# A router's first round on full arrays, and the order of the work behind it

## The chip, the cores and the metric

The kernel runs on one core of a Trainium2 chip. The metric is the device time of one execution in microseconds (us), as the median of several runs.

## The reference

Three layers follow each other on 4608 tokens. Attention with 32 memory slots per head gives x (4608 x 512). A mixture of eight experts follows: all (token, expert) scores are sorted, and each token goes to its best expert that still has room (576 tokens each). A dense layer pair with a gated ReLU6 ends the work.

```python
logits = x @ w_gate
for idx in np.argsort(-logits.flatten()):
    tok, e = idx // E, idx % E
    if assigned[tok] >= 0 or counts[e] >= cap:
        continue
    assigned[tok] = e; counts[e] += 1
for e in range(E):
    h = np.maximum(x[assigned == e] @ w1[e], 0.0)
    out[assigned == e] = h @ w2[e]
h = out @ w_in
y = (h * np.clip(h + 3.0, 0.0, 6.0) / 6.0) @ w_out
```

## The kernel before

Attention runs to about 190 us. It leaves the scores LG on the chip (128 partitions x 36 columns x 8 experts). The attention output x is written to memory as 36 tiles of 128 tokens. Eleven are done inside attention, and the other 25 by `x_tiles`, one half tile (one matmul group of 256 columns) at a time. Each finished tile is copied by ScalarE and written by SyncE's queue.

**The router** runs in eight rounds (`route(k)`), and each closes one expert. A round finds the expert that fills up first and the score at which it does. For that it searches the score's 32 bits in 8 steps of 4 bits (`for i in range(NST)`). In each step `cmp` (VectorE) marks in C which token's best score reaches which of 15 thresholds. TensorE multiplies C with the one-hot of the best expert, Bo, and so counts tokens per threshold and expert. FL says which counts reach 576, a matmul with ones broadcasts it, and VectorE makes the next thresholds. In round 0 the counting takes 36 matmuls, one for each token column, with 15 columns of the array. In later rounds it takes five matmuls over eight token columns each, with 128 columns. These leave an 8 x 8 block per pair of token columns, of which VectorE keeps the diagonal (CM, CR), and a further matmul with S8 folds it. After the search the round sums over partitions (`ce`, `tot`), turns every token's slot into a one-hot (`oh`, 36 columns in six pieces), and multiplies the pieces with token numbers to get the index list IDX. In round 0 VectorE makes five pieces and GpSimd the sixth (`ohp`). The x halves that remain are spread between those steps.

**Experts.** `weights` loads W1 and W2 of each expert (tensor number T, four chunks, by GpSimd's indirect DMA), squares them on ScalarE for a scale, and splits each into two half-precision tensors (ScalarE and VectorE). `gathers` fetches an expert's tokens, transposes them on TensorE (`xp`) and splits them (`xt`). `l1` is the first matmul layer, in groups of 48 matmuls over four banks for expert 0; `l2` is the second. A scale that all partitions need goes through `all_max`, a small matmul (`amx`) which takes one of the same four banks ("mm"). Experts go in pairs; `l34` then runs the dense layers for the pair's 1152 tokens.

**Dense weights** (32 pieces of 512 KB, 64-bit floats) are converted in the background by VectorE, ScalarE and GpSimd (tile `cva`): two pieces at a time, and four once expert 1's tokens are there (`spare`).

**What sets the order.** Every engine runs its list in order. The lists come from a small scheduler in the program itself: a clock `CK.now` that each matmul advances by a written cost, estimated busy times for VectorE, ScalarE and GpSimd (`V_.t`, `A_.t`, `G_.t`), and tasks that give up control until a time on this clock (`yield V_.t + HOP + LATE`). A time added to a `yield` makes no engine wait; it puts what follows later in the lists, behind whatever was written meanwhile. `need(cond)` lets the main line stand until a task has done its part; `l1` needs the expert's tokens, `l2` its second weights. On the chip an engine does wait where its next instruction's operand isn't there, and all behind it in its list waits too.

Of the kernel before, what the change touches and what calls it, by code (L numbers as in the profile page):

```python
# [9 lines left out]
F32 = mybir.dt.float32  # L10
# [10 lines left out]
def attn_moe_kernel(ctx: ExitStack, tc: tile.TileContext, q, k, v, phi, w_gate, w1, w2, w_in, w_out, out):  # L21
# [607 lines left out]

    MMQ = []  # L630

# [65 lines left out]
    def all_max(m, f, late=0.0):  # L697
        yield V_.t + HOP + late
        done = [False]
        while len(MMQ) >= 4 and not MMQ[0][0]:  # L700
            yield CK.now + 0.05
        p = mm_tile([128, 128], "amx", done)
        nc.tensor.matmul(p, m.bitcast(F32).to_broadcast([128, 128]), ident, start=True, stop=True)
        CK.now += 0.22
        yield CK.now + HOP
        V_.tensor_reduce(f, p, axis=AX.X, op=OP.max)
        done[0] = True

    def pow2(src, name, sq, lo, target, late=0.0):
# [11 lines left out]
        yield from all_max(m, f, late)  # L721
        SR[0] = SR[0] or sq
        f = f.bitcast(I32)
# [10 lines left out]
    IDX, EIX, SX = {}, {}, {}  # L734
    OHP = [False]
    SR = [False]
    R_OK = [0]
# [8 lines left out]
    def route(k):  # L746
        LATE = 0.0 if k < 2 else 1.6
        V = rt.tile([128, NT], F32, name="V")
# [3 lines left out]
        def best(c0, c1):  # L752
            n = c1 - c0
            L, v, b1, m = LG[:, c0:c1], V[:, c0:c1], B1[:, c0:c1], bm[:, c0:c1]
            V_.tensor_reduce(v, L, axis=AX.X, op=OP.max)
            V_.tensor_tensor(b1, L, v[:, :, None].to_broadcast([128, n, E]), op=OP.is_equal)
            V_.tensor_tensor(b1, b1, wE[:, None, :].to_broadcast([128, n, E]), op=OP.mult)
            V_.tensor_reduce(m, b1, axis=AX.X, op=OP.max)
            V_.tensor_tensor(Bo[:, c0:c1], b1, m[:, :, None].to_broadcast([128, n, E]), op=OP.is_equal)

        def cmp(C, TH, c0, c1):
# [8 lines left out]
        else:  # L770
            TH = TH0
            for i in range(NST):
                p = ps.tile([128, 64], F32, name="rtp")
                if k == 0:
                    due = []
                    for c0, c1 in ((0, 34), (34, NT)) if i == 0 else ((0, 18), (18, NT)):
                        if i == 0:
                            best(c0, c1)
                        cmp(C, TH, c0, c1)
                        due.append((c0, c1, V_.t))  # L780
                    if i > 1:
                        post()
                    if EM and i:
# [3 lines left out]
                        early()  # L787
                    x_tiles(3 if i else 4)
                    for c0, c1, v in due:
                        yield v + HOP  # L790
                        for t in range(c0, c1):
                            nc.tensor.matmul(p[:15, :E], C[:, t, 0:15], Bo[:, t], start=(t == 0), stop=(t == NT - 1))
                        CK.now += 0.0243 * (c1 - c0)
                    V_.t = max(V_.t, CK.now + HOP)
                    p1 = p
                else:
                    cmp(C, TH, 0, NT)
                    if i > 1:
                        post()
                    yield V_.t + HOP + LATE / 2  # L800
                    for t in range(0, NTP, 8):
                        nc.tensor.matmul(p, C[:, t:t + 8].rearrange("p t n -> p (t n)"),
                                         Bo[:, t:t + 8].rearrange("p t e -> p (t e)"),
                                         start=(t == 0), stop=(t == NTP - 8))
                    CK.now += 0.14
                    yield CK.now + HOP
                    V_.tensor_tensor(CM, p.rearrange("p (t e) -> p t e", t=8),
                                     MK[:, :, None].to_broadcast([128, 8, E]), op=OP.mult)
                    with nc.allow_low_precision(reason="integers up to 1152"):
                        V_.tensor_reduce(CR, CM.rearrange("p t e -> p e t"), axis=AX.X, op=OP.add)  # L810
                    yield V_.t + HOP + LATE / 2
                    p1 = ps.tile([128, 64], F32, name="rtp")
                    nc.tensor.matmul(p1[:, :E], S8, CR, start=True, stop=True)
                    CK.now += 0.03
                    yield CK.now + HOP
                r = slice(0, 128 if k else 15)
                V_.tensor_scalar(FL[r], p1[r, :E], float(CAP), None, op0=OP.is_ge)
                if k == 0:
                    x_tiles(1)
                yield V_.t + HOP  # L820
                p2 = ps.tile([128, 64], F32, name="rtp")
                nc.tensor.matmul(p2[:, :E], onesb[r], FL[r], start=True, stop=True)
                CK.now += 0.03
# [63 lines left out]
        if k == 0:  # L887
            x_tiles(4)
        yield V_.t + HOP + LATE
# [45 lines left out]
        def oh(q4):  # L935
# [3 lines left out]
            return o  # L939
        yield V_.t - 0.3  # L940
        OH = [oh(0)]
        if k == 0:
            lof = hbuf(2)[:, 0:6]
            G_.tensor_copy(lof, lo[:, 30:36])
            ohp = hbuf(1).bitcast(BF16)[:, 0:768].rearrange("p (t n) -> p t n", t=6)
            for t in range(6):
                G_.tensor_scalar(ohp[:, t], i128, lof[:, t:t + 1], None, op0=OP.is_equal)
            G_.t += 1.4
            OHP[0] = True
            x_tiles(7)  # L950
        for q4 in range(6):
            yield (G_ if k == 0 and q4 == 5 else V_).t + HOP + LATE
            if k == 0 and q4 == 4:
                OH.append(ohp)
            elif q4 < 5:
                OH.append(oh(q4 + 1))
            elif k:
                update()
# [5 lines left out]
            if k == 0:  # L964
                x_tiles(2 * NT if q4 == 2 else 2)
        yield CK.now + HOP
# [26 lines left out]
    def weights():  # L993
        for T in range(2 * E):
# [3 lines left out]
            for c in range(4):  # L998
                if T == 0 and c == 2:
                    while not OHP[0]:  # L1000
                        yield CK.now + 0.1
                w_issue(T, c)
                yield CK.now + 0.8, G_
# [14 lines left out]
            yield V_.t + HOP  # L1018
            s = yield from pow2(s4, f"s{which}_{k}", True, 0, (4, 13)[which], 1.5 if k > 1 else 0.0)
            (S1, S2)[which][k] = s  # L1020
# [44 lines left out]
    def gathers():  # L1065
        for k in range(E):
# [24 lines left out]
            for i in range(depth):  # L1091
                if k == 0 and i == 2:
                    while not SR[0]:
                        yield CK.now + 0.1
                fetch(i)
# [5 lines left out]
            for i in range(5):  # L1101
# [3 lines left out]
                done = [False]  # L1105
                while len(MMQ) >= 4 and not MMQ[0][0]:
                    yield CK.now + 0.05
# [154 lines left out]
    def x_tiles(n):  # L1262
        for _ in range(n):
# [7 lines left out]
            x_mm(t, ps, "mm", g)  # L1271
            CK.now += 0.435
            if g:
                x_ev(t)
                A_.t = max(A_.t, CK.now) + 0.5
                XC[0][0] = True
# [6 lines left out]
    def l1(k, carry=()):  # L1283
# [3 lines left out]
        for j0 in range(0, 8, G1):  # L1287
            need(lambda: k in XT)
            ps1 = []
            for j in range(j0, j0 + G1):  # L1290
                t = hbuf(j).bitcast(F16).rearrange("p (a n) -> p a n", a=2)
                HT[k].append(t)
                for a in range(2):
                    done = [False]
                    ps1.append((j, a, t, done, mm_tile([128, 288], "p1", done)))
                    if G1 == 1:
                        l1_mm(k, ps1, carry)
            if ps1:
                l1_mm(k, ps1, carry)
# [244 lines left out]
```

## Time and profile before

| | |
|---|---|
| median of 3 runs | 1480.12 us (1479.44 to 1480.93) |
| profiled execution | 1486.13 us, span 1484.3 us |
| TensorE matmul busy | 1368.3 us (92% of the span) |
| VectorE, ScalarE, GpSimd busy | 857.7, 731.7, 514.0 us |
| chain that ended last | TensorE 64%, VectorE 19%, waiting for nothing shown 6%, ScalarE 5% |

A busy time is the sum of an engine's instructions. The granted clock is the share of TensorE's full 2.4 GHz; 0.50 is its lower level, 1.2 GHz. In a timeline a line is an instruction or several merged ones (x6), with start, time from first to last, engine, source line, and in brackets how long the engine stood idle before and what released it. L619 and L568 are helpers that record most matmuls and most other instructions, so the tiles' names tell them apart.

### The profile page before, as it was taken

How to read it: one execution, taken by the hardware profiler on the slowest of the kernel's cores; microseconds unless marked ns; L12 is line 12 of the kernel's file. 1: busy time of each engine (PE TensorE's matmuls, PEld its weight loads, DVE VectorE, ACT ScalarE, POOL GpSimd, SP SyncE). 2: the span in 40 equal slices, each digit the busy share in tenths (PEclk: the TensorE clock that was granted, in tenths of full speed). 3: DMA queues.
4: the chain of work that ended last, by engine and by line, in shares of the span. 5: the costliest groups of instructions: out<-in, count | busy, mean ns of one | idle time of the engine just before them, and what ended most of it. 6: DMA issues, size and time to landing. Idle time of an engine off the chain costs nothing.

```text
span 1484.3 us, 25639 instructions
## 1 busy us (share of the span) xinstructions
PE 1368.3 (92%) x10170; PEld 925.4 (62%) x10170; DVE 857.7 (58%) x2018; ACT 731.7 (49%) x1419; POOL 514.0 (35%) x577
## 2 busy tenths in 40 slices
PE   4778785888899999999999999999999999999997
PEld 3667664767544555887555558885555589755553
DVE  4688966889997676652246766522469445221111
ACT  3677656559665364552334645524336545233332
POOL 5676304044465352310233523102335420023232
PEclk9999987899999999999999999999999999999999
DMA  9875486355420130320001303200013211000000
GB/s 296 297 252 193 138 257 229 120 177 174 141 85 22 48 120 1 107 65 1 1 22 57 111 1 107 65 1 1 22 48 120 72 51 50 1 1 22 1 22 22
DMA packets 65912, 130.65 MB, mean 88 GB/s; under 512 B 5248, under 2 KB 35968, under 8 KB 65792
## 3 DMA queue, kind: packets, MB, share of 16 engines
q1 hardware_dynamic: 49808, 74.48, 15.4%
q0 software_dynamic: 15168, 52.96, 11.0%
q8 instruction: 80, 1.31, 0.4%
q10 hardware_dynamic: 816, 1.57, 0.3%
q14 instruction: 40, 0.33, 0.1%
HBM read 110.12 MB, written 18.87 MB: 87 GB/s over the span
## 4 chain that ended last, share of the span: by engine, by line
PE 64%; DVE 19%; issue 6%; ACT 5%; DMA 3%; POOL 3%; ACTq 0%; SPq 0%; POOLq 0%; DVEq 0%
PE p L619 38%; PE acc L619 18%; DVE cva L568 4%; DVE w L568 2%; PE xa L420 2%; DMA xg<-xd,ix 2%; DVE h L568 1%; DMA wst<-in_moe_w_dram,ei 1%; POOL h L568 1%; PE kvp L191 1%; DVE ql L330 1%; PE xp L624 1%; ACT w L568 1%; ACT h L568 1%; DVE OH L568 1%
## 5 line engine op out<-in xcount | busy, mean ns | idle before, releaser
L619 PE MATMUL acc<-wo,h 128*128 128x512 f16 x1728 | 415.5, 380 | 8.3 <-DVE y L568 3.7
L619 PE MATMUL p<-yt,wi 128*128 128x384 f16 x2304 | 412.1, 327 | 0.0
L568 POOL TENSOR_TENSOR h<-h,h 128x384 f16<-128x384 f32 x192 | 187.0, 975 | 607.9 <-ACT h L568 466.3
L619 PEld LDWEIGHTS <-w 128*128 128x128 f16 x3072 | 339.5, 122 | 50.8 <-DVE w L568 5.3
L619 PEld LDWEIGHTS <-wi 128*128 128x128 f16 x2304 | 220.9, 98 | 162.7 <-issue 4.0
L619 PEld LDWEIGHTS <-h 128*128 128x128 f16 x1728 | 163.9, 98 | 178.6 <-issue 6.3
L568 ACT ACTIVATE h<-p,half_c,inv 128x384 f32<-128x384 f32 (+1 forms) x256 | 143.8, 587 | 265.5 <-PE p L619 262.1
L568 DVE SCALAR_TENSOR_TENSOR h<-h,p 128x384 f32<-128x384 f32 x192 | 105.7, 551 | 261.6 <-ACT h L568 258.6
L619 PE MATMUL p<-xt,w 128*128 128x288 f16 x1536 | 200.7, 290 | 2.5 <-DVE h L568 2.2
L619 PE MATMUL p<-h,w 128*128 128x288 f16 x1536 | 196.8, 288 | 5.0 <-DVE w L568 4.5
L568 ACT ACTIVATE h<-h 128x384 f16<-128x384 f32 x192 | 99.9, 521 | 131.0 <-DVE h L568 127.2
L568 POOL DMA_INDIRECT wst<-in_moe_w_dram,ei x64 | 71.1, 1110 | 119.2 <-DVE tot L568 36.3
L568 DVE SCALAR_TENSOR_TENSOR w<-wst,s,w 128x512 f16<-128x512 f32 x124 | 98.1, 823 | 1.0 <-ACT w L568 1.0
L568 DVE SCALAR_TENSOR_TENSOR h<-p,h 128x288 f16<-128x288 f32 x128 | 57.4, 453 | 64.2 <-ACT h L568 64.1
L568 ACT ACTIVATE h<-p 128x288 f16<-128x288 f32 x128 | 51.5, 408 | 86.9 <-PE p L619 86.9
L568 ACT ACTIVATE w<-wst,s 128x512 f16<-128x512 f32 x124 | 82.4, 712 | 7.0 <-DVE s L568 6.2
L568 DVE SCALAR_TENSOR_TENSOR cva<-dst,cva 128x512 int32<-128x512 int32 (+1 forms) x96 | 85.6, 915 | 0.4
L568 DVE TENSOR_REDUCE ym<-y 128x1 f32<-128x288 f32 x64 | 28.8, 449 | 92.7 <-ACT y L568 92.7
L568 ACT ACTIVATE wscr<-wst 128x1024 bf16<-128x1024 f32 x64 | 67.4, 1053 | 17.9 <-DMA wst<-in_moe_w_dram,ei 17.3
L568 ACT ACTIVATE y<-p 128x288 f32<-128x288 f32 x64 | 26.0, 407 | 99.7 <-PE p L619 98.9
L568 POOL DMA_INDIRECT xg<-xd,ix x35 | 35.9, 1026 | 70.6 <-PE xp L624 32.0
L191 PE MATMUL kvp<-kvt,A 128*64 128x128 f32 x576 | 43.6, 304 | 8.8 <-ACT A L170 4.2
(317 smaller groups left out, 1594.5 us busy)
## 6 DMA issues: line engine op xcount, KB each, us to landing
dst<-in_moe_w_out_dram SPq DMA_DIRECT2D x26, 512.0 KB, 3.7
qt<-in_q_dram SPq DMA_DIRECT2D x8, 1024.0 KB, 11.8
dq<-in_moe_w_in_dram SPq DMA_DIRECT2D x16, 512.0 KB, 4.9
xd<-xs SPq DMA_DIRECT2D x32, 256.0 KB, 4.5
kvt<-in_k_dram SPq DMA_DIRECT2D x7, 1152.0 KB, 9.6
kvt<-in_v_dram SPq DMA_DIRECT2D x7, 1152.0 KB, 11.9
dst<-in_moe_w_in_dram SPq DMA_DIRECT2D x15, 512.0 KB, 4.1
ph<-in_phi_dram SPq DMA_DIRECT2D x8, 576.0 KB, 10.6
```

Of the source, the lines that this page charges most:

```text
L191: nc.tensor.matmul(p[i * 64:(i + 1) * 64, g, 0:128], A[:, hp, r, :], KV[b][:, :, hp, r * 64:(r + 1) * 64], start=(r == 0), stop=(r == R - 1))
L330: nc.vector.scalar_tensor_tensor(QL[u][:, hs], QP[t], sq, QH[u][:, hs], op0=OP.mult, op1=OP.subtract)
L420: nc.tensor.matmul(p[r, g], AT[u][:, half, g, r], VB[b][:, g], start=True, stop=True)
L568: r = f(*a, **kw)
L619: nc.tensor.matmul(o, l, r, start=start, stop=stop)
L624: nc.tensor.transpose(o, i, idn)
```

## The change

- Round 0 counts as the later rounds do: five matmuls (`count`), CM and CR on VectorE, and the fold with S8.
- Each search step of round 0 issues six x halves (four, one and one; seven in the first step) where it issued four. Two stand behind the search, so none are left for the one-hots.
- All six one-hot pieces of round 0 are VectorE's. The waits on GpSimd's piece (`OHP`) and on the first scale (`SR`) go.
- `LOCK`: while `l1` of expert 0 takes its four banks, no scale and no token transpose takes one; and it starts when the first weight chunk is there.
- Round 1 gets later places: 0.4 more at two points in each search step, 2.4 at the sums and the first one-hot, 1.0 at each further one. Its one-hots come after expert 0's W2 is written. Expert 1's third to fifth gather wait for its first weights' chunks.
- The matmul of every weight scale comes 1.5 later; before, only from expert 2 on.
- The scheduler's costs of an x half and of its copy change (0.435 to 0.28; 0.5 to 1.05).

```diff
     def all_max(m, f, late=0.0):
-        while len(MMQ) >= 4 and not MMQ[0][0]:
+        while LOCK[0] or len(MMQ) >= 4 and not MMQ[0][0]:
             yield CK.now + 0.05
...
     def route(k):
-        LATE = 0.0 if k < 2 else 1.6
+        LATE, LS = ((0.0, 0.0), (2.4, 0.4), (1.6, 0.8))[min(k, 2)]
...
+        def count(p, c0, c1):
+            for t in range(c0, c1, 8):
+                nc.tensor.matmul(p, C[:, t:t + 8].rearrange("p t n -> p (t n)"),
+                                 Bo[:, t:t + 8].rearrange("p t e -> p (t e)"), start=(t == 0), stop=(t == NTP - 8))
+                CK.now += 0.028
...
-                    for c0, c1 in ((0, 34), (34, NT)) if i == 0 else ((0, 18), (18, NT)):
+                    for c0, c1 in ((0, 32), (32, NT)) if i == 0 else ((0, 16), (16, NT)):
...
-                    x_tiles(3 if i else 4)
+                    x_tiles(4 if i else 5)
                     for c0, c1, v in due:
                         yield v + HOP
-                        for t in range(c0, c1):
-                            nc.tensor.matmul(p[:15, :E], C[:, t, 0:15], Bo[:, t], start=(t == 0), stop=(t == NT - 1))
-                        CK.now += 0.0243 * (c1 - c0)
+                        count(p, c0, c1)
                     V_.t = max(V_.t, CK.now + HOP)
...
+                V_.tensor_tensor(CM, p.rearrange("p (t e) -> p t e", t=8),
+                                 MK[:, :, None].to_broadcast([128, 8, E]), op=OP.mult)
+                with nc.allow_low_precision(reason="integers up to 1152"):
+                    V_.tensor_reduce(CR, CM.rearrange("p t e -> p e t"), axis=AX.X, op=OP.add)
+                if k == 0:
+                    x_tiles(1)
+                yield V_.t + HOP + LS
+                p1 = ps.tile([128, 64], F32, name="rtp")
+                nc.tensor.matmul(p1[:, :E], S8, CR, start=True, stop=True)
...
         V_.tensor_copy(tot, sc[:, :, NT - 1])
         if k == 0:
-            x_tiles(4)
+            x_tiles(2)
...
+        while k == 1 and 0 not in W2:
+            yield CK.now + 0.1
         OH = [oh(0)]
         if k == 0:
-            lof = hbuf(2)[:, 0:6]
-            G_.tensor_copy(lof, lo[:, 30:36])
-            ohp = hbuf(1).bitcast(BF16)[:, 0:768].rearrange("p (t n) -> p t n", t=6)
-            for t in range(6):
-                G_.tensor_scalar(ohp[:, t], i128, lof[:, t:t + 1], None, op0=OP.is_equal)
-            G_.t += 1.4
-            OHP[0] = True
             x_tiles(7)
         for q4 in range(6):
-            yield (G_ if k == 0 and q4 == 5 else V_).t + HOP + LATE
-            if k == 0 and q4 == 4:
-                OH.append(ohp)
-            elif q4 < 5:
+            yield V_.t + HOP + (1.0 if k == 1 and q4 else LATE)
+            if q4 < 5:
                 OH.append(oh(q4 + 1))
...
     def weights():
-                if T == 0 and c == 2:
-                    while not OHP[0]:
-                        yield CK.now + 0.1
...
-            s = yield from pow2(s4, f"s{which}_{k}", True, 0, (4, 13)[which], 1.5 if k > 1 else 0.0)
+            s = yield from pow2(s4, f"s{which}_{k}", True, 0, (4, 13)[which], 1.5)
...
     def gathers():
             for i in range(depth):
-                if k == 0 and i == 2:
-                    while not SR[0]:
-                        yield CK.now + 0.1
+                while k == 1 and i > 1 and WC.get(2, (0,))[0] < i // 2:
+                    yield CK.now + 0.1
                 fetch(i)
...
     def x_tiles(n):
-            CK.now += 0.435
+            CK.now += 0.28
             if g:
                 x_ev(t)
-                A_.t = max(A_.t, CK.now) + 0.5
+                A_.t = max(A_.t, CK.now) + 1.05
...
     def l1(k, carry=()):
             need(lambda: k in XT)
+            need(lambda: k or 0 in WC)
+            LOCK[0] = k == 0
             ps1 = []
...
+            LOCK[0] = False
             if ps1:
                 l1_mm(k, ps1, carry)
```

## Rows read from the trace of the kernel before

**Rows 1.** The page, part 2: granted TensorE clock in 40 slices, tenths.
```profile
PEclk9999987899999999999999999999999999999999
```

**Rows 2.** Busy by stretch: length, engines, clock, DMA share, GB/s; sum: 242 to 445.
```profile
329.00:385.00 56.00, 51.45 (x400) 44.47 (x399) 54.46 (x98) 44.42 (x88) 23.26 (x19) 0.94 0.57 188
385.00:445.00 60.00, 50.96 (x260) 26.41 (x258) 59.38 (x90) 41.70 (x74) 35.72 (x25) 0.91 0.32 97
sum 203.00, PE 166.20 PEld 123.11 DVE 186.23 ACT 131.62 POOL 84.89; mean PE 33.24 PEld 24.62 DVE 37.25 ACT 26.32 POOL 16.98
...
700.00:800.00 100.00, 99.67 (x588) 53.53 (x587) 40.27 (x109) 38.32 (x73) 28.42 (x31) 1.00 0.02 9
```

**Rows 3.** Timeline, one warm search step of round 0.
```profile
222.47 1.05 PE L792 MATMUL rtp<-Bo,C 128*15 128x8 bf16 x36
...
224.09 0.17 PE L822 MATMUL rtp<-FL,onesb 15*128 15x8 bf16 x1
224.19 1.56 PE L420 MATMUL xa<-vb,ats 128*128 128x256 f32 x6
...
225.68 1.05 PE L792 MATMUL rtp<-Bo,C 128*15 128x8 bf16 x36
```

**Rows 4.** Timeline, the same chain in round 1; last, its five counting matmuls.
```profile
249.46 0.21 DVE L568 TENSOR_TENSOR CM<-rtp,MK 128x64 f16<-128x64 f32 x1
...
249.71 0.26 DVE L568 TENSOR_REDUCE CR<-CM 128x8 f16<-128x64 f16 x1
...
250.03 0.19 PE L813 MATMUL rtp<-CR,S 128*128 128x8 f16 x1 [2.99 <-DVE s_0m L568]
...
250.26 0.17 DVE L568 TENSOR_SCALAR FL<-rtp 128x8 bf16<-128x8 f32 x1 [0.23 <-PE rtp L813]
...
272.29 0.32 PE L802 MATMUL rtp<-Bo,C 128*128 128x64 bf16 x5 [1.00 <-DVE C L568]
```

**Rows 5.** Stretches of half a microsecond in round 0's search, columns as in rows 2.
```profile
199.00:199.50 0.50, 0.50 (x22) 0.43 (x19) 0.47 (x5) 0.00 (x0) 0.00 (x0) 0.79 1.05 426
...
209.50:210.00 0.50, 0.50 (x15) 0.35 (x15) 0.00 (x0) 0.25 (x1) 0.00 (x0) 0.97 0.65 49
```

**Rows 6.** Timeline, round 0 after its search: sums and one-hots.
```profile
231.11 0.17 DVE L568 CAST tot<-scn 128x2 bf16<-128x2 f32 x1
...
232.49 0.21 PE L891 MATMUL rtp<-tot,tri 128*128 128x2 bf16 x1
...
234.66 7.06 POOL L568 TENSOR_SCALAR h<-i,h 128x128 bf16<-128x128 bf16 x6
...
235.00 4.61 DVE L568 TENSOR_TENSOR OH<-lo,i 128x768 bf16<-128x768 int32 x5
...
241.78 0.18 PE L961 MATMUL rtp<-RH,h 128*128 128x10 bf16 x1 [0.40 <-POOL h L568]
```

**Rows 7.** Timeline, start of expert 0's layer one: gather, weight split, matmul.
```profile
245.55 1.17 POOL L568 DMA_INDIRECT h<-xd,ix  x1 [1.30 <-DVE bm L568]
...
251.50 2.56 ACT L568 ACTIVATE w<-wst,s 128x512 f16<-128x512 f32 x4 [2.14 <-DVE s L568]
...
260.24 0.32 PE L619 MATMUL p<-xt,w 128*128 128x288 f16 x1
```

**Rows 8.** Timeline, TensorE in expert 0's layer two, VectorE's last token split.
```profile
312.97 0.31 PE L961 MATMUL rtp<-RH,OH 128*128 128x10 bf16 x6 [2.73 <-DVE dmm L568]
...
321.32 0.63 PE L624 MATMUL xp<-ident,xg 128*128 128x128 f32 x4 [1.42 <-DMA xg<-xd,ix]
...
328.64 0.48 DVE L568 SCALAR_TENSOR_TENSOR xt<-xp,sx,xt 128x256 f16<-128x256 f32 x1 [0.25 <-ACT xt L568]
...
330.87 3.96 PE L619 MATMUL p<-xt,w 128*128 128x288 f16 x31
```

**Rows 9.** Timeline, TensorE at expert 1's layer two and the first dense layers.
```profile
361.93 23.85 PE L619 MATMUL p<-h,w 128*128 128x288 f16 x175 [4.15 <-DVE w L568]
...
396.50 0.77 PE L703 MATMUL amx<-ident,sy_1m 128*128 128x128 f32 x2 [5.84 <-DVE sy_1m L568]
```

More of the change, by code (lines that the diff above doesn't have):

```diff
@@ L628, in fp16 @@
         return max(0.027, n / 2400.0 + 0.003)
-    MMQ = []
+    MMQ, LOCK = [], [False]
     def mm_slot(done):
@@ L721, in pow2 @@
         yield from all_max(m, f, late)
-        SR[0] = SR[0] or sq
         f = f.bitcast(I32)
@@ L734, in attn_moe_kernel @@
     IDX, EIX, SX = {}, {}, {}
-    OHP = [False]
-    SR = [False]
     R_OK = [0]
@@ L787, in route @@
                         early()
-                    x_tiles(3 if i else 4)
+                    x_tiles(4 if i else 5)
                     for c0, c1, v in due:
                         yield v + HOP
-                        for t in range(c0, c1):
-                            nc.tensor.matmul(p[:15, :E], C[:, t, 0:15], Bo[:, t], start=(t == 0), stop=(t == NT - 1))
-                        CK.now += 0.0243 * (c1 - c0)
+                        count(p, c0, c1)
                     V_.t = max(V_.t, CK.now + HOP)
-                    p1 = p
                 else:
@@ L799, in route @@
                         post()
[L800 to L805, printed above, removed]
-                    yield CK.now + HOP
[L807 to L814, printed above, removed]
+                    yield V_.t + HOP + LS
+                    count(p, 0, NT)
+                    yield CK.now + HOP
+                V_.tensor_tensor(CM, p.rearrange("p (t e) -> p t e", t=8),
[4 more added lines that the diff above has]
+                    x_tiles(1)
+                yield V_.t + HOP + LS
+                p1 = ps.tile([128, 64], F32, name="rtp")
+                nc.tensor.matmul(p1[:, :E], S8, CR, start=True, stop=True)
+                CK.now += 0.03
+                if k == 0:
+                    V_.t = max(V_.t, CK.now + HOP)
+                else:
                     yield CK.now + HOP
-                r = slice(0, 128 if k else 15)
-                V_.tensor_scalar(FL[r], p1[r, :E], float(CAP), None, op0=OP.is_ge)
+                V_.tensor_scalar(FL, p1[:, :E], float(CAP), None, op0=OP.is_ge)
                 if k == 0:
@@ L821, in route @@
                 p2 = ps.tile([128, 64], F32, name="rtp")
-                nc.tensor.matmul(p2[:, :E], onesb[r], FL[r], start=True, stop=True)
+                nc.tensor.matmul(p2[:, :E], onesb, FL, start=True, stop=True)
                 CK.now += 0.03
@@ L964, in route @@
             if k == 0:
-                x_tiles(2 * NT if q4 == 2 else 2)
+                x_tiles(2 * NT)
         yield CK.now + HOP
@@ L1105, in gathers @@
                 done = [False]
-                while len(MMQ) >= 4 and not MMQ[0][0]:
+                while LOCK[0] or len(MMQ) >= 4 and not MMQ[0][0]:
                     yield CK.now + 0.05
```

## The prediction

> **What bounds the kernel now.** I read the 40-slice page first: the granted clock is below full only in the sixth to eighth slice, 186 to 297 us [rows 1]. Then the table by stage [rows 2]: from 700 us on TensorE is busy 99.67 of 100 us, so a delay or gain made earlier is simply carried to the end. From 242 to 445 us VectorE is busy 186.23 of 203 us, and 59.38 of 60 in the last part. So two things can move the total: when the first router round hands over (about 242 us), and how much of 242 to 445 VectorE (16.8 us idle) and TensorE (36.8 us idle) lose by waiting for each other. Last I read the timeline there, instruction by instruction.
>
> All arithmetic is on the profiled execution: 1486.13 us, span 1484.3. The median of the runs shown is 1480.12, that is 6.0 us (0.4%) less; I carry the difference over to the median.
>
> **First round, search steps.** A warm step runs from one block of 36 counting matmuls (1.05 us) to the next: 225.68 - 222.47 = 3.21 us [rows 3]. TensorE has no gap in it: six matmuls, which are three x halves, take 1.56 us, so a half is 0.52 and four are 2.08. The new step has six halves and a longer chain. Counted from the broadcast matmul of the flags: 0.10 for that, four halves 2.08, five wide counting matmuls 0.32, then the two new VectorE operations until the folding matmul starts, 250.03 - 249.46 = 0.57, then folding matmul 0.23 and flags 0.15 with a handover of 0.2, together 0.58, beside which the half queued behind the folding matmul runs [rows 4]. Sum 3.65, against 3.21: +0.45. Ends: 3.5 if TensorE never waits for the fold, 3.9 if each half is in the way. Seven steps: +3.2 (2.0 to 4.8). VectorE's dense maximum and the new thresholds stay beside the four halves. The DMAs grow to three 256 KB x writes and one 512 KB load a step, 1.28 MB in 3.65 us or 350 GB/s, below the 426 GB/s that one half microsecond shows [rows 5]; SyncE's queue gets the x writes sooner, each behind the load that waits for VectorE, as now. The first step gets the same fold and one more half in the stretch of low clock: +1.0.
>
> **Clock.** It falls to half at about 199.3 us and comes back at 209.5 [rows 5], although TensorE worked all that time; the 36 matmuls that use 15 columns are part of what it did. With full arrays it may come back sooner. No row shows by how much; the ends are 0 and one warm step's work, 3.2. I take half, -1.6, as nothing lies nearer.
>
> **Tail of the first round.** The prefix matmul starts at 232.49, 1.2 us after its operand ended (231.11 + 0.17), because four slow x halves are queued ahead. After the change one half is left, which runs in the pause before: -1.0. The one-hots: GpSimd's six end at 241.72 and the last matmul of the round starts at 241.78, while VectorE was done with five at 239.61 [rows 6]. At 0.92 each a sixth there ends at 240.5: -1.2. The Trainium skill, page "Perfetto Trace Analysis", section "Optimizing Scalar/DVE Operations", says that work may be better off on another engine when VectorE is saturated. By it the sixth one-hot would cost 0.9 instead of giving 1.2. The trace differs: VectorE stands idle from 239.61, so at this place it isn't saturated.
>
> Sum of the first round: 3.2 + 1.0 - 1.6 - 1.0 - 1.2 = +0.4, so its index is ready at about the same time (-3 to +3). Six halves a step only change where the x work stands.
>
> **Start of layer one.** What changes is behind the index. Two of four weight loads of expert 0 no longer wait for the one-hots, and the last x tile is written earlier, some 7 us by my sum. The first token gather starts at 245.55 [rows 7], 3 us after the index; now it starts directly: -2.5. The scaled weights start at 251.50, released by a scale that waited for those late loads. That wait goes, and VectorE's update and next best-expert pass (some 3 us) are next ahead of it, then the scale's matmul, now queued 1.5 us later: -1.5. Layer one's first matmul, 260.24, needs both; with gathers and conversions less bunched I take -4 (ends -1.5 and -6).
>
> **Layers of expert 0.** The second round's one-hots, scale matmuls and token transposes sit in TensorE's queue among layer two, and where their operand is late the layer waits behind them: 2.73 and 1.42 us are the large ones [rows 8]. Queued later, these go; keeping the four banks of layer one together saves about as much again at the scale matmul that now takes one of them. One-hots behind the second weights help these too. The lock itself only orders: a scale or transpose comes after the four banks are taken, at worst one group of 48 matmuls later (6.1 us at 3.96 / 31 [rows 8]), and nothing on another engine stands behind it. The new guard on expert 1's third to fifth gather holds GpSimd's list, with expert 1's second weight loads behind it; their conversion is over by then, so it costs nothing, or up to 3 us if not. Together -4 (ends 0 and -7). Layer two of expert 0 would end at 330.9 - 8 = 323.
>
> **What is late next.** The same delays put expert 1's tokens off. The last token split ends at 328.64 + 0.48 = 329.1, 1.7 us before layer one of expert 1 starts at 330.87 [rows 8]: there is no slack. The diff adds, in the scheduler's time, 2 x 0.4 in each of 8 steps, 2 x 2.4 at the two sums, 2.4 + 5 x 1.0 at the one-hots: 18.6 us. The whole frame stands 8 us earlier, so the tokens are ready at 329.1 + 18.6 - 8 = 340, and TensorE waits 17 us from 323. Layer one of expert 1 starts 9 us later than before. Ends: 0 (the delays elapse while VectorE is behind anyway) and +13.
>
> **What is paid back.** While TensorE waits, VectorE converts dense weights, which otherwise hold up the next stages. Layer two of expert 1 waits 4.15 us for its weights and the dense layers 5.84 for a scale queued on VectorE [rows 9]; each is followed by a stretch at the lower clock. A granted 0.94 over 56 us and 0.91 over 60 [rows 2] are 6.7 and 10.8 us at half, which lose 3.4 and 5.4. With 9 us more both waits go nearly whole, and with them I count half of that loss: 4.2 + 4.8 + 4 = 13; smaller waits in the dense layers, 1. So 9 - 14 = -5 (ends -12 and +9). In VectorE's terms: its idle time shrinks from 16.8 to about 12, which is what lay idle around those late one-hots. From 460 us on nothing differs, but for scales of the first two experts queued 1.5 later, which costs nothing where TensorE has other matmuls ahead.
>
> Forecast: 1480.1 - 5 = 1475 (1481 for an execution like the profiled one).
>
> **Rivals.** *The wait isn't paid back (slower).* While expert 1's tokens are missing, only two conversion buffers are free, so VectorE may idle along with TensorE. Then 9 us of delay stand against 4.2 + 2 for the weights at most, or against nothing where these, loaded after the gathers, slide along: +3 to +9, 1486. It decides from the point where VectorE is busy under some 70% of TensorE's wait. For it: the buffers, and no slack in rows 8. Against it: 186 of 203 us busy, with low-priority work always at hand.
>
> *No wait arises.* VectorE's queue runs behind the scheduler's clock already (the 5.84 us), so the added delays may elapse without being seen. Then -8 is carried, and some of the later waits shrink: -11, 1469. Against it: 18.6 is much more than any lag in the rows.
>
> *It cancels.* VectorE sets the pace to 445 us whatever TensorE does, and its work after the handover is the same; its idle time stays near 16.8. Then 1480. For it: 59.38 of 60 us busy. This also covers a change that doesn't do what it says: a search 0.45 us a step longer, with the clock coming back as late as before.
>
> **Numbers.** Forecast case (-3 to -8, so 1472 to 1477) 0.40; no wait 0.16; cancels 0.20; not paid back 0.24. A measurement of this kernel can tell 0.2%, 3 us, from no change. Faster 0.56, same 0.20, slower 0.24. The range takes in most of the outer cases: 1467 to 1486.
>
> **What would show it.** Search steps of 3.6 to 3.7 us with six halves; the clock back before 209; last one-hot matmul near 240.7; first token gather right behind the index, layer one near 256; no 2.7 us wait in layer two of expert 0; then a wait of 10 to 20 us before layer one of expert 1, with VectorE over 80% busy in it; the two waits of rows 9 under 2 us. I'm wrong if that wait is there and VectorE idles in it, if layer one doesn't start earlier, or if TensorE's waits after 360 us stay as they were.

## The result, and the profile after

The changed kernel takes 1492.41 us (median, 1489.68 to 1495.07) beside 1481.01 us of the kernel before on the same chip: a ratio of 1.0069, 95% interval 1.0055 to 1.0082, or 10.2 us slower. It lies outside the forecast's range, 1467 to 1486, and the forecast itself was 1475. The profiled execution of after took 1493.21 us, its span is 1491.4.

Part 2 of the page has the clock lowest in the seventh slice (224 to 261 us, 0.5), and at 0.8 in the ninth to eleventh, 298 to 410 us, where it was 0.9 or more before [rows 1]. The busy time by stretch (length, TensorE, weight load, VectorE, ScalarE, GpSimd, clock, DMA share, GB/s) answers to [rows 2]:

```profile
PEclk9999995988899999999999999999999999999999
```

```profile
329.00:385.00 56.00, 43.37 (x291) 36.34 (x292) 49.44 (x81) 39.70 (x78) 29.76 (x21) 0.79 0.55 174
385.00:445.00 60.00, 53.66 (x319) 31.72 (x318) 59.42 (x91) 41.76 (x74) 30.57 (x23) 0.94 0.31 97
...
700.00:800.00 100.00, 99.67 (x596) 55.25 (x595) 38.87 (x105) 36.36 (x69) 26.17 (x29) 1.00 0.02 9
```

From 329 to 385 us TensorE has lost 8 us against before; at 700 nothing differs. TensorE's timeline shows where (start, duration, engine, line, operation, idle before it and what ended that). First a warm search step [rows 3], the end of the first round [rows 6] and the start of layer one [rows 7]:

```profile
221.75 0.31 PE L760 MATMUL rtp<-Bo,C 128*128 128x64 bf16 x5
...
225.07 0.31 PE L760 MATMUL rtp<-Bo,C 128*128 128x64 bf16 x5
...
230.62 0.16 PE L891 MATMUL rtp<-tot,tri 128*128 128x2 bf16 x1 [1.20 <-DVE tot L568]
...
238.46 0.33 PE L954 MATMUL rtp<-RH,OH 128*128 128x10 bf16 x6 [0.55 <-DVE OH L568]
...
253.00 0.67 PE L619 MATMUL p<-xt,w 128*128 128x288 f16 x2
```

A step takes 3.32 us, and layer one of expert 0 begins 7.2 us earlier than before. Then the end of expert 0 and the tokens of expert 1 [rows 8]; the last layer-two matmul ends at 317.3:

```profile
315.81 1.51 PE L619 MATMUL p<-h,w 128*128 128x288 f16 x11
...
322.36 0.77 PE L703 MATMUL amx<-ident,sy_0m 128*128 128x128 f32 x2 [3.49 <-DVE sy_0m L568]
...
332.10 1.09 PE L624 MATMUL xp<-ident,xg 128*128 128x128 f32 x4 [8.04 <-DMA xg<-xd,ix]
336.51 1.09 PE L624 MATMUL xp<-ident,xg 128*128 128x128 f32 x4 [3.33 <-DMA xg<-xd,ix]
...
341.49 3.81 PE L619 MATMUL p<-xt,w 128*128 128x288 f16 x15
```

GpSimd's timeline in that wait: the tokens are fetched from 327.98, and expert 1's second weights only behind them, from 340.61. The last line is the kernel before, where these start at 327.15:

```profile
327.98 1.62 POOL L568 DMA_INDIRECT xg<-xd,ix  x1 [2.17 <-DVE ix L568]
329.90 4.04 POOL L568 DMA_INDIRECT xg<-xd,ix  x1 [0.30 <-issue]
...
340.61 0.94 POOL L568 DMA_INDIRECT wst<-in_moe_w_dram,ei  x1 [2.93 <-DMA xg<-xd,ix]
```

```profile
327.15 0.94 POOL L568 DMA_INDIRECT wst<-in_moe_w_dram,ei  x1 [2.22 <-DMA xg<-xd,ix]
```

Behind the wait, layer one of expert 1 starts at the lower clock, 0.50 until about 345.6 us; in the kernel before it starts at 1.00. The columns are length, TensorE, clock, DMA share and GB/s:

```profile
341.49:343.50 2.01, 2.01 (x10) 0.50 0.59 116
```

And the two waits of [rows 9], which were to go. The one before the second weights is now two, 2.38 and 2.16; the one before the scale is 5.23. The last line is the third round's first count, which stands at nearly the same place among the dense matmuls in every kernel (732 to 736 matmuls behind the start of expert 1's layer one), and in before comes at 465.32:

```profile
373.29 1.62 PE L619 MATMUL p<-h,w 128*128 128x288 f16 x6 [2.38 <-DVE w L568]
377.07 3.14 PE L619 MATMUL p<-h,w 128*128 128x288 f16 x13 [2.16 <-DVE w L568]
...
408.94 0.77 PE L703 MATMUL amx<-ident,sy_1m 128*128 128x128 f32 x2 [5.23 <-DVE sy_1m L568]
...
473.54 0.31 PE L760 MATMUL rtp<-Bo,C 128*128 128x64 bf16 x5
```

Executions differ by some us already where the first round starts (its first count lies between 196.18 and 200.71 us), so the kernels are also compared by two lengths read from such lines, in one profile each. **A** runs from the first round's last one-hot matmul to layer one of expert 1, **B** from there to the third round's first count. The difference in us is (ratio - 1) x 1481; each ratio is to the kernel before on the same chip (e1 to e4, e5 to e8, e9 to e11 and e12 to e14 ran on four). Kernels that differ little (before and e10; e1, e8 and e9) spread by under 2 us in A and by under 1 in B.

| kernel | ratio to before (95%) | us | A | B |
|---|---|---|---|---|
| before | 1 | 0 | 89.1 | 134.5 |
| after | 1.0069 (1.0055-1.0082) | +10.2 | 103.0 | 132.1 |
| e1 no delays | 0.9987 (0.9976-0.9999) | -1.9 | 89.3 | 133.8 |
| e2 before + delays | 1.0086 (1.0066-1.0106) | +12.7 | 107.5 | 128.7 |
| e3 e1, scales early | 1.0032 (1.0019-1.0045) | +4.7 | 92.4 | 135.7 |
| e4 after, scales early | 1.0079 (1.0066-1.0092) | +11.7 | 104.8 | 133.4 |
| e5 after, own buffers | 1.0043 (1.0029-1.0057) | +6.4 | 100.9 | 130.1 |
| e6 after, half delays | 1.0045 (1.0027-1.0063) | +6.7 | 98.0 | 133.9 |
| e7 e1, four halves | 1.0048 (1.0031-1.0064) | +7.1 | 97.0 | 133.5 |
| e8 e1, no lock | 0.9985 (0.9975-0.9994) | -2.2 | 89.9 | 133.0 |
| e9 e1, sy_1 later | 0.9977 (0.9959-0.9996) | -3.4 | 91.1 | 133.4 |
| e10 before, sy_1 later | 1.0005 (0.9986-1.0024) | +0.7 | 87.4 | 134.5 |
| e11 e1, splits on VectorE | 0.9950 (0.9935-0.9966) | -7.4 | 89.0 | 128.8 |
| e12 e5, splits on VectorE | 1.0011 (0.9995-1.0028) | +1.6 | 103.0 | 124.2 |
| e13 before, splits on VectorE | 0.9989 (0.9971-1.0007) | -1.6 | 88.4 | 133.4 |
| e14 after, splits on VectorE | 1.0050 (1.0032-1.0068) | +7.4 | 104.1 | 128.7 |

After against before, A is 13.9 longer and B 2.4 shorter.

### The profile page after: what moved, and what is told of

Its sections match the earlier page's. It is cut to its first block, busy times and chain, and to the rows that moved or that the text cites. A ratio compares the mean times of both kernels' runs of the same rounds, so it can differ in the third digit from the quotient of the medians.

```text
span 1491.4 us, 25164 instructions
## 1 busy us (share of the span) xinstructions
PE 1361.9 (91%) x9930; PEld 918.7 (62%) x9930; DVE 860.9 (58%) x2035; ACT 733.2 (49%) x1419; POOL 509.9 (34%) x570
## 3 DMA queue, kind: packets, MB, share of 16 engines
q8 instruction: 78, 1.28, 0.3%
## 4 chain that ended last, share of the span: by engine, by line
PE 58%; DVE 12%; issue 5%; DMA 4%; POOL 3%; ACT 2%; POOLq 0%; DVEq 0%; ACTq 0%
PE p L619 38%; PE acc L619 18%; DVE cva L568 4%; DVE w L568 2%; DMA wst<-in_moe_w_dram,ei 2%; DMA xg<-xd,ix 1%; DVE h L568 1%; POOL h L568 1%; PE xp L624 1%; ACT w L568 1%; ACT h L568 1%; DVE OH L568 1%; POOL wst L568 1%; DVE C L568 0%; POOL out_dram L568 0%
## 5 line engine op out<-in xcount | busy, mean ns | idle before, releaser
L568 ACT ACTIVATE h<-h 128x384 f16<-128x384 f32 x192 | 100.1, 521 | 130.1 <-DVE h L568 126.7
L568 DVE SCALAR_TENSOR_TENSOR cva<-dst,cva 128x512 int32<-128x512 int32 (+1 forms) x96 | 82.6, 881 | 1.6 <-ACT dst L568 0.8
L568 ACT ACTIVATE y<-p 128x288 f32<-128x288 f32 x64 | 26.0, 407 | 101.6 <-PE p L619 100.9
L191 PE MATMUL kvp<-kvt,A 128*64 128x128 f32 x576 | 43.3, 303 | 9.1 <-ACT A L170 4.2
```

What stands on the lines that cost most here:

```text
L191: nc.tensor.matmul(p[i * 64:(i + 1) * 64, g, 0:128], A[:, hp, r, :], KV[b][:, :, hp, r * 64:(r + 1) * 64], start=(r == 0), stop=(r == R - 1))
L568: r = f(*a, **kw)
```

## The experiments

**Which part costs the time: e1 to e4.** e1 takes the second round's delays out of the changed kernel; e2 puts them alone into the kernel before.

```diff
-        LATE, LS = ((0.0, 0.0), (2.4, 0.4), (1.6, 0.8))[min(k, 2)]
+        LATE, LS = ((0.0, 0.0), (0.0, 0.0), (1.6, 0.8))[min(k, 2)]
...
-            yield V_.t + HOP + (1.0 if k == 1 and q4 else LATE)
+            yield V_.t + HOP + LATE
```

```diff
-        LATE = 0.0 if k < 2 else 1.6
+        LATE, LS = ((0.0, 0.0), (2.4, 0.4), (1.6, 0.8))[min(k, 2)]
...
-                    yield V_.t + HOP + LATE / 2
+                    yield V_.t + HOP + LS
...
-            yield (G_ if k == 0 and q4 == 5 else V_).t + HOP + LATE
+            yield (G_ if k == 0 and q4 == 5 else V_).t + HOP + (1.0 if k == 1 and q4 else LATE)
```

> The second round's added delays are set to nothing (0.4, 2.4 and 1.0 become 0); all else is as in the changed kernel. Theory A (the delays cost the time, since the index of expert 1 comes 10.7 us later and its gathers, its second weights and the dense scale all hang behind it): layer one of expert 1, which starts at 341.49 us in the changed kernel, starts at 325 to 330, the wait before it is under 6 us, and the time falls by 10 or more, to 1476 to 1482. Theory B (the later scales and the closed banks hold the weights and tokens of expert 1 back, whatever the delays): it starts at 335 or later and the time stays above 1487. Theory C (VectorE's work up to 470 us sets the end): the start moves, the time moves by less than 3.

> The kernel before, with the second round's delays of the change alone. Theory A: index, gathers and layer one of expert 1 come 16 to 18 us later than before (330.87 becomes 347 to 349), 4 or 5 us of it are returned in the dense layers, and the time is 1493 to 1496. The prediction's own term (what is late is paid back by the two later waits): those waits, 4.15 and 5.84, are under 2 us each and the time is 1484 to 1486. Theory B: within 3 us of the kernel before.

Measured: 1480.32 us and 1493.75 us. Without the delays 12.1 us go from the changed kernel; with them alone the kernel before becomes 12.7 us slower. Theory A stands: in e1 with its numbers (layer one of expert 1 at 326.77), in e2 with its time, though layer one starts at 345.71 and not at 347 to 349. B and C fall as causes of the loss. TensorE's timeline at expert 1's layer one, first in e1, then in e2:

```profile
324.27 0.63 PE L624 MATMUL xp<-ident,xg 128*128 128x128 f32 x4 [0.89 <-DMA xg<-xd,ix]
326.21 0.77 PE L703 MATMUL amx<-ident,sy_0m 128*128 128x128 f32 x2 [1.31 <-DVE sy_0m L568]
326.77 1.65 PE L619 MATMUL p<-xt,w 128*128 128x288 f16 x6
```

```profile
329.35 0.32 PE L961 MATMUL rtp<-RH,OH 128*128 128x10 bf16 x6 [3.90 <-DVE OH L568]
336.32 1.08 PE L624 MATMUL xp<-ident,xg 128*128 128x128 f32 x4 [6.66 <-DMA xg<-xd,ix]
...
345.71 2.50 PE L619 MATMUL p<-xt,w 128*128 128x288 f16 x15
...
377.71 20.88 PE L619 MATMUL p<-h,w 128*128 128x288 f16 x169 [0.98 <-DVE w L568]
...
410.24 0.77 PE L703 MATMUL amx<-ident,sy_1m 128*128 128x128 f32 x2 [6.27 <-DVE sy_1m L568]
```

In e2 A grows by 18.4, near the scheduler's 18.6. From e1 to after it grows by 13.7 only: the second round's last one-hot matmul comes 10.7 later, counted from the first round's last, and 3.0 are added behind it, where the second token gather holds GpSimd 4.04 (0.95 in e1). Why 18.6 of delay is 17.9 at that matmul in e2 and 10.7 in after is open. Of the two waits that the prediction's term wanted under 2 in e2, the one before the second weights came so (0.98), the one before the scale didn't (6.27). e3 and e4 put the weight scales of the first two experts back to their earlier place, without and with the delays:

```diff
-            s = yield from pow2(s4, f"s{which}_{k}", True, 0, (4, 13)[which], 1.5)
+            s = yield from pow2(s4, f"s{which}_{k}", True, 0, (4, 13)[which], 1.5 if k > 1 else 0.0)
```

> As the run without delays, and the weight scales of the first two experts are queued 1.5 earlier again, as before. What is left of the change is its first round, the closed banks and the guards. Theory A: little more than without the delays alone, within 2 us of it. Theory B: another 4 us or more less, and then the handover of the first round, 3 to 7 us earlier than before, is seen whole: 1473 to 1476.

> The changed kernel with only the weight scales of the first two experts queued 1.5 earlier again. Theory A: the index of expert 1 keeps its place (327.7 us), layer one of expert 1 stays at 341, the time within 2 us of the changed kernel. Theory B: layer two of expert 0 and the scale of expert 1's first weights come earlier and the time falls by 4 us or more.

Measured: 1486.55 and 1493.91. e4 is as Theory A said: 1.5 us from after, layer one of expert 1 at 341.27. Neither theory forecast e3: it is 6.6 us slower than e1 (A 3.1 and B 1.9 longer). So without the delays the later scales help. In e3 TensorE waits 6.81 us at the scale matmul of expert 0's first weights, which stands ahead of the tokens; how much of the 6.6 hangs on this wait isn't shown:

```profile
244.67 0.77 PE L703 MATMUL amx<-ident,s_0m 128*128 128x128 f32 x2 [6.81 <-DVE s_0m L568]
```

**Why it isn't paid back: e5 and e6.** In e5 three of expert 1's token gathers land in hidden-layer buffers, so the second weights needn't wait for the tokens to leave theirs; the guard on those gathers becomes another one, which looks at expert 0's layer two. e6 halves the delays.

```diff
-                    xg = big[-1][:, i % 2]
+                    xg = hbuf(3 + i)[:, 0:512]
...
-                while k == 1 and i > 1 and WC.get(2, (0,))[0] < i // 2:
+                while k == 1 and i > 1 and L2D.get(0, 0) < 4:
...
-            while k not in EIX or T == 3 and 1 not in XI:
+            while k not in EIX:
...
-                    if i and T + 1 < 2 * E and T != 2:
+                    if i and T + 1 < 2 * E:
```

```diff
-        LATE, LS = ((0.0, 0.0), (2.4, 0.4), (1.6, 0.8))[min(k, 2)]
+        LATE, LS = ((0.0, 0.0), (1.2, 0.2), (1.6, 0.8))[min(k, 2)]
...
-            yield V_.t + HOP + (1.0 if k == 1 and q4 else LATE)
+            yield V_.t + HOP + (0.5 if k == 1 and q4 else LATE)
```

> The changed kernel, in which expert 1's third to fifth token gather no longer land in the staging buffers of the weights but in hidden-layer buffers that are free by then; so the second weights of expert 1 are loaded as soon as each first weight is split, ahead of or between the gathers. Theory D (nothing is paid back because those loads slide along with the gathers): they start at 326 to 333 us instead of 340.61, the weights are split while TensorE waits, the two waits of 2.38 and 2.16 us before layer two of expert 1 go, the wait of 5.23 before the dense layers shrinks to 2 or less, and the time falls by 5 to 9, to 1484 to 1488. Theory E (the loads are not it: VectorE, ScalarE and GpSimd work in written order, and what is written there behind the token splits stands still too): the 2.38 and 2.16 go, but the wait before the dense layers grows by as much, and the time stays within 3 us of the changed kernel.

> The changed kernel with half of each added delay (1.2, 0.2 and 0.5 for 2.4, 0.4 and 1.0). Theory A, with nothing paid back: the cost of 12.1 us for 18.6 of delay is a slack of some 2 to 4 and then one for a little under one; half the delay puts layer one of expert 1 at 333 to 336 us and the time at 1485 to 1487. A payback that only covers a few us (the prediction's term, too large but real) would swallow the first half: 1480 to 1483. Theory B has no forecast here.

Measured: 1487.91, so 3.8 us of the loss come back, and 1487.65 for e6: half the delay costs 8.6 of the 12.1, and all of that lies in A (98.0 against 89.3), with nothing back in B. That is Theory A's way, a little past its numbers (layer one of expert 1 at 337.51, A said 333 to 336). e5's time is at the edge of Theory D's range; the fall of 3.8 lies between D's 5 and E's 3, and not all of D's rows came. Its loads start at 322.48 and 333.11, one wait of 2.54 is left where there were two, and the scale's wait is still 5.25:

```profile
322.48 1.15 POOL L568 DMA_INDIRECT wst<-in_moe_w_dram,ei  x1 [7.26 <-DVE eo L568]
...
333.11 1.20 POOL L568 DMA_INDIRECT wst<-in_moe_w_dram,ei  x1 [0.30 <-issue]
```

```profile
369.68 1.68 PE L619 MATMUL p<-h,w 128*128 128x288 f16 x11 [2.54 <-DVE w L568]
...
403.00 0.77 PE L703 MATMUL amx<-ident,sy_1m 128*128 128x128 f32 x2 [5.25 <-DVE sy_1m L568]
```

**Parts of the first round: e7 and e8.**

Both are edits of e1.

```diff
-                    x_tiles(4 if i else 5)
+                    x_tiles(2 if i else 3)
```

```diff
-            LOCK[0] = k == 0
+            LOCK[0] = False
```

> The kernel without the delays, and with four x halves a search step in place of six (three in the first step's first place in place of five), as the kernel before had them. The prediction's own sum: a step falls from 3.32 us to about 3.0, but as many x halves are left over for the end of the round, ahead of the one-hots; the sum is 0 to +3 us, 1480 to 1484. Rival (x work is hidden in the steps only while the halves are short of the step's chain): the step stays at 3.2 or more, the leftover is added whole, 16 halves of 0.5: +5 to +8, 1485 to 1488.

> The kernel without the delays, and without the lock that keeps scale matmuls and token transposes from taking one of the four banks of layer one of expert 0. The prediction counted about 1.5 us for the lock: 1481 to 1483, with a wait of TensorE for a bank in layer one of expert 0. Rival (the lock orders and no more): within 1.5 us of the kernel without the delays, 1479 to 1482.

Measured: 1488.97 and 1480.00. Without the delays the lock does nothing that can be measured (e8). e7's rival is the nearer (9.0 us over e1, still more than it said): a step is 3.19 instead of 3.32, so there was little to win, and the halves left over run in lumps between the one-hots, after which the first gather, which needs all of x, is 5.7 us behind the last one-hot matmul (1.0 in e1).

```profile
233.01 3.70 PE L420 MATMUL xa<-vb,ats 128*128 128x256 f32 x16
...
238.76 0.31 PE L954 MATMUL rtp<-RH,OH 128*128 128x10 bf16 x6 [0.56 <-DVE OH L568]
```

```profile
244.44 0.96 POOL L568 DMA_INDIRECT h<-xd,ix  x1 [10.91 <-DVE CM L568]
```

**What sets B: e9 to e14.** The wait before sy_1m was 5 to 6.5 us in nearly every kernel. e9 (on e1) and e10 (on before) queue that matmul 6.0 later. e11 (on e1) gives VectorE four splits of expert 1's second weights.

```diff
-        sy = yield from pow2(a, f"sy_{k}", False, 15, 2, 3.0 * (k % 2 and k > 1))
+        sy = yield from pow2(a, f"sy_{k}", False, 15, 2, (0.0, 6.0, 0.0, 3.0)[k % 2 + 2 * (k > 1)])
```

```diff
-    PS = {3: (0, 2, 4, 6)}
+    PS = {}
```

> The kernel without the delays, and the scale matmul of expert 1's output (sy_1m), before which TensorE has waited 5 to 6.5 us in nearly every kernel so far, stands 6.0 of the scheduler's time later in TensorE's order. Theory F (that wait is made by the written order: a matmul whose operand VectorE delivers late stands ahead of dense matmuls that are ready, so nothing done earlier pays it back): the wait falls under 1 us, the dense matmuls go on, and the time falls by 3 to 6, to 1474 to 1477. Theory C (VectorE's work sets the pace up to 450 us, and TensorE waits for it in one place or another): the wait moves to the evictions and dense weights of the following blocks, the time stays within 2 us of the kernel without the delays.

> The kernel before with only that one scale matmul 6.0 later. Theory F: the wait of 5.84 us goes, the time falls by 3 to 6 us against the kernel before, 1476 to 1479. Theory C: within 2 us of the kernel before.

> The kernel without the delays, and four splits of expert 1's second weights that GpSimd made (with two operations of ScalarE each) go to VectorE: 4 x 0.75 = 3.0 us more for VectorE between 345 and 385 us, where it is busy 39.3 of 40. Theory C (VectorE's work sets the pace there, which is why a lead of TensorE of some 6 us at layer one of expert 0 is worth 1.7 at the end): +2.5 to +4, 1483 to 1484. Theory F: within 1.5 us, since the four splits also come without GpSimd's queue.

Measured: 1479.66, 1482.59 and 1475.32. The scale's wait is a symptom: moved out of the way, an equal one stands at a matmul of the dense layers (e9; in e10 one of 3.56):

```profile
399.02 3.60 PE L619 MATMUL acc<-wo,h 128*128 128x512 f16 x8 [5.99 <-ACT h L568]
```

Theory F falls. So does C, in the other direction: with 3.0 us more for VectorE, which is busy 39.90 of 40 us from 345 to 385, e11 is 5.5 us faster than e1. For these four splits a chain of two ScalarE operations (0.73 and 0.64) and a GpSimd one (1.18 to 1.59) becomes one ScalarE operation (0.77) and one of 0.74 on VectorE. Expert 1's last split ends 34.9 us behind the start of its layer one in e1 and 29.7 behind it in e11, and the waits of 1.90 and 2.88 before the second weights become 0.48 and 0.49. What part of this is the shorter chain and what part the work taken off GpSimd wasn't tried apart. First e1, then e11:

```profile
356.31 0.91 PE L619 MATMUL p<-h,w 128*128 128x288 f16 x6 [1.90 <-DVE w L568]
360.09 2.26 PE L619 MATMUL p<-h,w 128*128 128x288 f16 x8 [2.88 <-DVE w L568]
...
360.89 0.74 DVE L568 SCALAR_TENSOR_TENSOR w<-wst,s,w 128x512 f16<-128x512 f32 x1
```

```profile
354.51 0.54 PE L619 MATMUL p<-h,w 128*128 128x288 f16 x3 [0.48 <-DVE w L568]
355.54 6.72 PE L619 MATMUL p<-h,w 128*128 128x288 f16 x51 [0.49 <-DVE w L568]
...
354.75 1.40 DVE L568 SCALAR_TENSOR_TENSOR w<-wst,s,w 128x512 f16<-128x512 f32 x2
```

The Trainium skill, page "Perfetto Trace Analysis", section "Optimizing GPSIMD Operations", prefers other engines to GpSimd where there is one; e11 agrees, by 5.5 us. Its section "Optimizing Scalar/DVE Operations" says that taking work off a saturated VectorE may make sense; here the busy share misleads, since 26.80 of the 39.90 us in e11 are dense conversions (tile `cva`), which can wait. The last three put the same change into e5 (e12), before (e13) and after (e14).

> The changed kernel, delays and all, with the token buffers of e5 and the four splits on VectorE of e11. Theory G (the path after the wait is the load, scale and split of expert 1's second weights; loads that go ahead of the tokens and a shorter chain of splits let the wait be used): layer two of expert 1 follows layer one without a wait over 1 us and the time is 1480 to 1483. Theory C' (the wait itself is the loss, whatever comes behind it): each repair gives what it gave alone, 4.5 and 0 to 1, 1486 to 1488.

> The kernel before with the four splits on VectorE alone. If the first round's lead of some 3 to 6 us at layer one of expert 0 is lost in front of expert 1's second weights, the move gains less here than the 5 us it gained without the delays, 1480 to 1482 (2 or less), and the lead is worth 5 or more once that path is short. If the lead is lost elsewhere, the move gains the same 5 here: 1476 to 1478.

> The changed kernel with the four splits on VectorE alone. Theory G: the waits of 2.38 and 2.16 us before layer two of expert 1 go and the time falls by 4 to 6, 1486 to 1488. Theory C': within 2 us of the changed kernel.

Measured: 1483.21, 1481.02, 1488.66. e12 is 8.6 us below after: the two repairs add up (3.8 in e5, 2.8 in e14), at the edge of Theory G's range and with its row: layer two of expert 1 follows without a wait, 105 matmuls on end. e14 alone falls by 2.8, between the 2 of Theory C' and the 4 of Theory G; of the two waits one of 1.02 is left.

```profile
365.15 13.02 PE L619 MATMUL p<-h,w 128*128 128x288 f16 x105
```

In e13 the move gains 1.6 (not certain: its interval reaches 1), so e11 and e13 are 5.8 us apart: with that chain short, the change without its delays is worth 5.8 us and not 1.9. The dense conversions go with this. VectorE's operations on tile `cva` (busy, count, clock, DMA share, GB/s) in A and in B, for before, after, e13, e11 and e12:

```profile
242.00:331.00 89.00, 8.02 (x13) 0.87 0.48 156
331.00:465.00 134.00, 93.36 (x115) 0.94 0.37 118
```

```profile
239.00:341.50 102.50, 16.64 (x27) 0.78 0.44 141
341.50:473.50 132.00, 84.86 (x101) 0.93 0.34 108
```

```profile
236.00:324.60 88.60, 7.98 (x13) 0.83 0.50 162
324.60:458.00 133.40, 93.04 (x115) 0.97 0.39 119
```

```profile
237.40:326.40 89.00, 11.90 (x19) 0.86 0.49 154
326.40:455.20 128.80, 87.37 (x110) 0.96 0.37 118
```

```profile
236.00:338.90 102.90, 17.45 (x29) 0.78 0.47 149
338.90:463.10 124.20, 79.17 (x99) 0.99 0.33 109
```

B is clearer when it is parted at the first dense matmul (`p<-yt,wi`): ahead of it lie expert 1's two layers, behind it the dense layers up to the count, with the conversions that are still left for them. The lines are the conversions behind that matmul, before and after:

```profile
385.62:465.32 79.70, 58.00 (x67) 0.94 0.24 73
```

```profile
399.16:473.54 74.38, 41.60 (x48) 0.95 0.15 46
```

| kernel | conversions in A | expert 1's layers | dense layers in B | conversions left for these |
|---|---|---|---|---|
| before | 13 | 54.8 | 79.7 | 67 |
| e13, short chain | 13 | 49.0 | 84.4 | 75 |
| e1 | 19 | 56.5 | 77.3 | 60 |
| e11, short chain | 19 | 50.5 | 78.3 | 65 |
| after | 27 | 57.7 | 74.4 | 48 |
| e14, short chain | 27 | 51.9 | 76.8 | 56 |
| e5, own buffers | 29 | 55.7 | 74.4 | 48 |
| e12, both | 29 | 49.8 | 74.5 | 54 |
| e2 | 27 | 52.7 | 76.0 | 54 |

The short chain takes 5.7 to 6.0 us off expert 1's layers in all four pairs. In this table the dense layers take 74 to 77 us with 48 to 60 conversions left, 78 to 80 with 65 to 67, and 84.4 with 75. So dense work done early does come back, in the dense layers: 5.3 us from before to after. There expert 1's own layers get 2.9 longer (2.1 of it TensorE's busy time at a granted clock of 0.90 and not 0.94), and 2.4 are left. In e13 the 5.8 gained ahead of the dense layers goes again for want of early conversions. This is read from the traces; no run changed the early conversions alone. Nor does it fill the delay: from e11 to e12 A grows by 14.0 and B falls by 4.6. e2 departs from after: its second weights are loaded as late (344.80, 0.9 ahead of layer one), but split in time, so its layers are 5.0 shorter than after's. Why is open.

## Why the prediction was wrong

**The step that failed is "What is paid back".** It counted 14 us returned for 9 us late, and after returns 2.4 (B against before) for 13.9. The frame was right: a wait, and the slow rival names the mechanism that came (loads that slide along), but prices it at +3 to +9. By its terms:

- The waits of 4.2 and 4.8 were to go. They are 4.54 (2.38 and 2.16) and 5.23.
- Half of the loss at the lower clock, 4, was to come back. The wait adds to it: behind it (TensorE busy 7.42 of 24.19 us) layer one of expert 1 starts at 0.50 for some 4 us, and expert 1's layers run at 0.90 where before ran at 0.94.
- Smaller waits in the dense layers, 1, came out larger: these layers are 5.3 shorter, 0.6 of it the scale's wait.
- It took VectorE's busy share in the wait as the test. From 316 to 342 us VectorE is busy 20.26 of 26, 78%, above the 70% named as the turning point, and still only 2.4 is returned: it did expert 1's first weight splits, output and token splits, which had come late themselves. From index to layer one it runs 1 dense conversion; before it ran 4.
- The wait before the second weights is no lack of VectorE time but a chain: gathers, loads into the same buffers, scale, three-operation splits. It slides with the tokens (e5) and is too long by itself (e11, e14); with both mended expert 1's layers are 7.9 shorter than in after (e12).
- The wait before sy_1m moves when it is moved (e9). That it is TensorE's share of a later limit, the dense conversions, is argued from the table above and not shown.

**What is late next.** Right in place, short in size: layer two of expert 0 ends at 317.3 and not 323, so TensorE waits 24 us with some matmuls in between, not 17. That layer one of expert 1 starts near 340 as said (341.49) is in part luck: after's first round ends 3.3 us earlier than in the profile of before, and counted from that end layer one is 13.9 late, not 9.

**Search steps.** +0.45 was forecast, 3.32 - 3.21 = +0.11 came. TensorE has almost no gap (0.1 us a step); it is six halves of 0.49 (1.97 for the four behind the flags), 0.31 of counting and the small matmuls. The added VectorE chain, which the sum put behind the others, is hidden. (In that sum the flags' 0.15 is 0.17 in rows 4, and no row shows the handover of 0.2.) **Tail of the first round.** From prefix matmul to last one-hot matmul 7.8 us instead of 9.3, so -1.5 for -1.2, and the prefix no longer waits behind x halves.

**Clock.** It is back at 202.5 (0.58, then 1.00), not 209.5, as hoped; but that isn't shown to be the full arrays' doing. e10, with the old round, has it back by 201.5, and the same old round takes 40.3, 41.0 and 39.4 us in e2, e10 and e13 from first count to last one-hot matmul, 43.3 in the profile of before. That profile was an unlucky one: about 3 of the 6 us that the prediction spread over the whole kernel lay in the very round that was changed. The new round takes 40.3 in after, and 39.0 to 40.8 in the ten other kernels with six halves. The forecast of about no change holds.

**Start of layer one.** Right: the gather starts 1.0 us behind the last one-hot matmul (3.8), layer one 14.5 (18.5), so -4. **Layers of expert 0.** The matmuls did leave layer two; in e1, where they stay, the lead of 4.5 at layer one is 1.3 at layer two, and A is the same as before. Between the two TensorE stands idle 9.8 us in e1 and 5.6 before; 4.2 of it lie at three matmuls of the second round that stand directly ahead of layer two and wait for VectorE (1.71, 1.28 and 1.20). No run moved these. The lock, priced with half of that step, does nothing without the delays (e8).

## What to carry over

In these kernels work done in a wait came back where it was the next stages' own (5.3 us in the dense layers), while a stage whose own chain slid with the wait got longer (2.9). So follow that chain (buffer, load, scale, split), and don't read the return from the busy share of an engine that always has filler to do. A wait can cost clock on top: here the clock stood at 0.50 for 4 us behind it. Delays that a scheduler adds to one chain come out as time to a large part, not always whole: of 18.6 planned, A grew by 18.4 (before to e2) and 13.7 (e1 to after), of 9.3 by 8.7 (e1 to e6). The version to keep is e11, without the delays and with the splits on VectorE: 1475.32 us, 0.9950 of before.

## What was not expected

The clock's return lies between 201.4 and 209.5 us in four executions of the same old first round (before, e2, e10, e13), 4.7 to 11.0 us behind its first count. And one token gather of expert 1 held GpSimd 4.04 us in after and e14, 4.06 in e2 and 2.93 in e4 (2.21 in e5 and e12), where the others take 0.94 to 1.62; what holds it is open.
